# Local attention and two MLPs: attention's q, k and v loaded two units ahead instead of one

## The chip, the cores and the metric

The kernel runs on one core of one Trainium2 chip. The metric is the device time of one execution in microseconds. The kernel before took 663.96, 665.17 and 665.17 us in three runs; the median is 665.17 us. One more execution was taken with a profile, and all rows below come from it.

## What is computed

Three layers follow each other, in float32. The first is attention over 2 batches, 8 heads, 768 positions and 64 columns a head; a query sees the first `n_global` (8) keys and the last `n_local` (96) keys, with a bias that grows with the distance:

```python
scores = scale * np.matmul(q, k.transpose(0, 1, 3, 2))
keep = is_global | is_local          # pos < n_global, or 0 <= rel < n_local
bias = -slopes[:, None, None] * dist[None, :, :]
scores = np.where(keep, scores + bias, -1000000000.0)
a = np.exp(scores - scores.max(-1)); a = a / (a.sum(-1) + 1e-09)
x = np.matmul(a, v)                  # (2, 8, 768, 64) -> (1536, 512)
```

Then two MLPs work on its 1536 rows of 512 columns:

```python
g = x @ w_gate                       # 512 -> 1536
x = (g * sigmoid(g) * (x @ w_val)) @ w_out
h = x @ w_in                         # 512 -> 2048
out = (h * np.cos(h)) @ w_out2
```

The weights arrive as 64-bit floats; the chip's engines take 32 bits, so the kernel also converts them.

## The kernel before, in words

Attention is cut into 12 units. A unit is one of three chunks of 512 query rows (four tiles of 128 rows) with one of four pairs of heads. A unit needs q (128 x 512 floats), the gathered windows of k (128 x up to 744) and of v (128 x 8 x 128). `load(u)` (L560) issues them on SyncE's DMA queue (SP); v comes last. q and k have two buffers in turn, v has three. Unit 0 is loaded ahead of everything, in the prologue.

The loop of `attn_fast` (L687) goes through steps s. A unit has two groups of two tiles, 24 groups in all, and group g is handled over several steps:

- `S_(g)` in step g: the score matmuls on TensorE (PE, L597), then the bias, the row minimum and the exponential on VectorE (DVE, L610) and ScalarE (ACT, L613).
- `R_(g)` and `N_(g)` in step g + 1: the reciprocal of the row sums on DVE, and the division by them on GpSimd (POOL, L626).
- `T_(g)` and `V_(g)` in step g + 3: transposes on PE (L638), copies out of the banks on DVE or ACT (L644), and the value matmuls on PE (L660).
- `X_(g)` in step g + 4: the split of a finished unit into a high and a low part, the input of the first MLP (L396, L400).

q is scaled on POOL by `scale(u)` (L579) before a unit's scores: in step 2u - 1, for u from 1. In one step PE's order is transposes, scores, value matmuls. Every engine works through its own list in the order of the program, and so does SP: an instruction that waits holds all behind it.

Between attention's instructions a small planner (`bg_all`, `bg_fill`) puts the conversion of the weights, a piece at a time. Each piece is a 1 MB load of raw 64-bit words (`load64`, L174), some operations on ACT and DVE that end with L240, and a 512 KB store of the converted tile to memory (`store32`, L245), from which it is read again later. These loads and stores go through the same SP queue as q, k and v. The next raw load is issued right behind the store. The planner counts estimated engine times; `load(u)` tells it of a transfer with `self.dma(1.1)`.

After attention, PE runs the two MLPs almost without a gap, each product as three matmuls of high and low parts (L385 to L387).

The line numbers are those of the kernel before.

Of the kernel before, what the change touches and what calls it, by code (L numbers as in the profile page):

```python
# [18 lines left out]
F32 = mybir.dt.float32  # L19
# [10 lines left out]
CT = 512  # L30
# [3 lines left out]
KC = 744  # L34
# [120 lines left out]
class Body:  # L155
# [399 lines left out]
    def attn_fast(self, p, sc, tr, pv):  # L555
        nc, d = self.nc, self.d
        units = [(c, k) for c in range(NCH) for k in range(NPAIR)]
        op, P, sums, nmins, ptb, pvb = {}, {}, {}, {}, {}, {}

        def load(u):  # L560
            c, k = units[u]
            q = p.tile([128, CT], F32, tag="q", bufs=2, name="q")
            kk = p.tile([128, KC], F32, tag="k", bufs=2, name="kk")
            v = p.tile([128, 8, 128], F32, tag="v", bufs=3, name="v")
            at = 0
            for b in sorted({b for b, _ in TILES[c]}):
                ii = [i for bb, i in TILES[c] if bb == b]
                w = 128 * len(ii)
                nc.sync.dma_start(out=q[:, at:at + w], in_=d["qT"][b, k, :, 128 * ii[0]:128 * ii[0] + w])
                at += w  # L570
            nc.sync.dma_start(out=kk[:, :KW[c]], in_=d["kw"][c, k, :, :KW[c]])
            nc.sync.dma_start(out=v, in_=d["vw"][c, k])
            self.dma(1.1)
            op[u] = (q, kk, v)

        def scale(u):

            q, k = op[u][0], units[u][1]
            nc.gpsimd.tensor_scalar(out=q, in0=q, scalar1=self.qscale[:, k:k + 1], scalar2=1.0,  # L579
                                    op0=ALU.mult, op1=ALU.mult)  # L580
# [7 lines left out]
        def S_(g):  # L588

            u, c, k, tiles = grp(g)  # L590
            q, kk, _ = op[u]
            bank = [sc(), sc()]
            self.at("pe", sum(t[2] for t in tiles) / 500, (), [id(b) for b in bank])
            for i, (t, off, w, vb) in enumerate(tiles):
                for h in range(2):
                    a = slice(64 * h, 64 * h + 64)
                    nc.tensor.matmul(bank[h][:, 256 * i:256 * i + w], lhsT=q[a, 128 * t:128 * t + 128],  # L597
                                     rhs=kk[a, off:off + w], start=True, stop=True)
            sums[g] = p.tile([128, 4], F32, tag="sum", bufs=6, name="sum")
            nmins[g] = p.tile([128, 4], F32, tag="nmin", bufs=6, name="nmin")  # L600
            for i, (t, off, w, vb) in enumerate(tiles):
                dist = self.base[:, 0:128] if w == 128 else self.base[:, 128:128 + WW]
                for h in range(2):
                    n = 2 * i + h
                    pt = p.tile([128, WW], F32, tag="P", bufs=PB, name="P")
                    slope = 2.0 ** -(2 * k + h + 1)
                    nm = nmins[g][:, n:n + 1]

                    self.at("d", w / 700, [id(bank[h])], [("P", g, n)])
                    nc.vector.tensor_tensor_reduce(out=pt[:, :w], in0=bank[h][:, 256 * i:256 * i + w], in1=dist,  # L610
                                                   scale=slope, scalar=3.0e38, op0=ALU.add, op1=ALU.min, accum_out=nm)
                    self.at("a", w / 500, [("P", g, n)], [("P", g, n)])
                    nc.scalar.activation(out=pt[:, :w], in_=pt[:, :w], func=AF.Exp, scale=-1.0, bias=nm,  # L613
                                         accum_out=sums[g][:, n:n + 1])
                    P[g, n] = pt

        def R_(g):
            self.at("d", 0.35, [("P", g, 3)], [("R", g)])
            nc.vector.tensor_scalar_add(sums[g], sums[g], 1.0e-9)
            nc.vector.reciprocal(sums[g], sums[g])  # L620

        def N_(g):
            for i, (t, off, w, vb) in enumerate(grp(g)[3]):
                for n in (2 * i, 2 * i + 1):
                    self.at("g", w / 400, [("R", g)], [("P", g, n)])
                    nc.gpsimd.tensor_scalar(out=P[g, n][:, :w], in0=P[g, n][:, :w], scalar1=sums[g][:, n:n + 1],  # L626
                                            scalar2=1.0, op0=ALU.mult, op1=ALU.mult)

        def T_(g):

            for i, (t, off, w, vb) in enumerate(grp(g)[3]):
                bank = tr()
                nk, nb = (128, 1) if w == 128 else (KB, 2)
                self.at("pe", 0.11 * 2 * nb, [("P", g, 2 * i), ("P", g, 2 * i + 1)], [id(bank)])
                for h in range(2):
                    for j in range(nb):
                        o = 128 * (nb * h + j)
                        nc.tensor.transpose(bank[:nk, o:o + 128], P[g, 2 * i + h][:, nk * j:nk * j + nk], self.ident)  # L638
                    del P[g, 2 * i + h]
                pt = ptb[g, i] = p.tile([128, 512], F32, tag="PT", bufs=PTB, name="PT")  # L640

                e = "a" if self.t["a"] <= self.t["d"] else "d"
                self.at(e, 0.16 + nb * 0.21, [id(bank)], [("E", g, i)])
                (nc.scalar.copy if e == "a" else nc.vector.tensor_copy)(pt[:nk, :256 * nb], bank[:nk, :256 * nb])  # L644

        def V_(g):

            u, c, k, tiles = grp(g)
            v = op[u][2]
            if g % 2 == 0:  # L650
                pvb[u] = pv()
            self.at("pe", 0.25 * sum(len(t[3]) for t in tiles), [("E", g, 0), ("E", g, 1)], [id(pvb[u])])
            for i, (t, off, w, vb) in enumerate(tiles):
                nk = 128 if w == 128 else KB
                pt = ptb.pop((g, i))
                for j, bl in enumerate(vb):
                    for h in range(2):
                        a = slice(64 * h, 64 * h + 64)
                        o = 128 * (len(vb) * h + j)
                        nc.tensor.matmul(pvb[u][a, 128 * t:128 * t + 128], lhsT=v[:nk, bl, a], rhs=pt[:nk, o:o + 128],  # L660
                                         start=j == 0, stop=j == len(vb) - 1)

        def X_(g):

            u, c, k, _ = grp(g)
            if g % 2 == 0:
                return lambda: None
            xt, ps = self.xtile(c, k), pvb.pop(u)
            self.x[c].append(xt)
            self.split_hi(xt, ps)  # L670
            return lambda: self.split_lo(xt, ps)
# [9 lines left out]
        for _ in range(4):  # L681
            nc.tensor.matmul(bank[:, :232], lhsT=zero[:, :128], rhs=zero[:, :232], start=True, stop=True)
        load(1)
        self.bg_start()
        self.distances(p)

        for s in range(NG4 + LAG + 1):  # L687
            self.wr_free = 3 if s > 1 + LAG else 2 if s > 1 else 0
            low = X_(s - LAG - 1) if s > LAG else None
            if LAG <= s < NG4 + LAG:  # L690
                T_(s - LAG)
            if s < NG4:
                if s % 2 == 1 and s // 2 + 1 < len(units):
                    scale(s // 2 + 1)
                S_(s)

            if 1 <= s <= NG4:
                R_(s - 1)
                N_(s - 1)
            if low:  # L700
                low()
            if LAG <= s < NG4 + LAG:
                V_(s - LAG)
            if s % 2 == 0 and 0 < s // 2 < len(units) - 1:
                load(s // 2 + 1)
            yield s

    def attn_general(self, p, banks):
# [199 lines left out]
```

## Time and profile before

| | |
|---|---|
| median of three runs | 665.17 us (663.96 to 665.17) |
| the profiled execution's own time | 664.43 us |
| its span (first to last instruction) | 662.6 us |
| mean granted TensorE clock | 0.993 of full speed |
| PE busy | 635.3 us, 96% of the span |
| DVE, ACT, POOL busy | 66%, 59%, 9% |
| bytes moved | 88.95 MB, mean 134 GB/s |
| attention | from the start to about 97 us |

How to read it: the times in the rows are microseconds from the start of the span. A row of a timeline gives the start, the duration, the engine, the line of the program, the operation, the tiles written and read, and how many instructions were merged; in brackets stands how long the engine was idle before it, and what it waited for. A DMA's issue on SP is short; its data lands later.

### The profile page before, as it was taken

Reading aid. Unit: us, or ns where it says so; the run is one execution under the profiler, and the core shown is the slowest. Engines: PE = TensorE matmul, PEld = TensorE weight load, DVE = VectorE, ACT = ScalarE, POOL = GpSimd, SP = SyncE. Lnnn points to the kernel's source line nnn. Section 1 sums busy time; section 2 is a strip of 40 time slices with the busy share of each in tenths; the row PEclk is TensorE's granted clock in tenths of the full one; section 3 lists DMA queues with packets and bytes.
Section 4 is the critical chain, followed back from the end, with each engine's and each line's share of the span. In section 5 each row is a group of like instructions: output and inputs, shape, how many; then the busy total and the mean of one; then the engine's idle time right before and its main releaser. Section 6 shows DMA issues by size and latency. Waiting matters only on the chain.

```text
span 662.6 us, 8727 instructions
## 1 busy us (share of the span) xinstructions
PE 635.3 (96%) x3176; PEld 517.2 (78%) x3176; DVE 436.8 (66%) x769; ACT 392.7 (59%) x670; POOL 56.7 (9%) x112
## 2 busy tenths in 40 slices
PE   5997989999999999999999998999999999999996
PEld 3674768888888888788888887888888888888885
DVE  4899698787787775557788638766554444554442
ACT  3887575555555454335665348877666665655562
POOL 1676560000000000000000000000000000000000
PEclk9999799999999999999999999999999999999999
DMA  7665425555555455567767442331010000010001
GB/s 261 240 206 212 148 78 208 191 191 194 197 196 197 168 208 196 195 234 258 255 242 251 164 157 65 127 96 32 1 63 1 1 0 1 0 64 0 1 1 68
DMA packets 22658, 88.95 MB, mean 134 GB/s; under 512 B 2640, under 2 KB 3920, under 8 KB 18256
## 3 DMA queue, kind: packets, MB, share of 16 engines
q1 hardware_dynamic: 22176, 88.06, 38.4%
q8 instruction: 27, 0.44, 0.3%
q10 hardware_dynamic: 432, 0.26, 0.1%
q14 instruction: 23, 0.19, 0.1%
HBM read 67.34 MB, written 20.97 MB: 133 GB/s over the span
## 4 chain that ended last, share of the span: by engine, by line
PE 87%; DVE 5%; DMA 3%; ACT 2%; issue 1%; POOL 1%; POOLq 0%; DVEq 0%
PE bank L387 27%; PE bank L385 27%; PE bank L386 27%; PE bank L660 2%; PE bank L597 2%; DMA kk<-in_kw 2%; PE bank L638 2%; DVE P L610 1%; DMA q<-in_qT 1%; DVE PT L644 1%; POOL P L626 0%; DVE x L400 0%; DVE wr L240 0%; DVE w L224 0%; ACT r L475 0%
## 5 line engine op out<-in xcount | busy, mean ns | idle before, releaser
L385 PE MATMUL bank<-x,w 128*128 128x512 f32 x336 | 130.8, 389 | 0.0
L387 PE MATMUL bank<-x,w 128*128 128x512 f32 x336 | 130.7, 389 | 0.0
L386 PE MATMUL bank<-x,w 128*128 128x512 f32 x336 | 130.7, 389 | 0.0
L477 DVE SCALAR_TENSOR_TENSOR u<-r,bank 128x512 f32<-128x512 f32 x48 | 33.0, 688 | 82.3 <-ACT r L475 82.3
L385 PEld LDWEIGHTS bank<-x,w 128*128 128x128 f32 x336 | 63.1, 188 | 13.2 <-issue 0.2
L387 PEld LDWEIGHTS bank<-x,w 128*128 128x128 f32 x336 | 63.1, 188 | 13.1
L386 PEld LDWEIGHTS bank<-x,w 128*128 128x128 f32 x336 | 63.1, 188 | 13.1
L474 ACT ACTIVATE r<-bank,cst 128x512 f32<-128x512 f32 x48 | 33.0, 688 | 47.8 <-PE bank L387 47.8
L387 PE MATMUL bank<-x,big 128*128 128x512 f32 x144 | 56.1, 390 | 1.8 <-DVE big L224 1.8
L385 PE MATMUL bank<-t,w 128*128 128x512 f32 x144 | 56.1, 390 | 0.9 <-ACT w L209 0.9
L387 PE MATMUL bank<-t,w 128*128 128x512 f32 x144 | 56.2, 390 | 0.5 <-DVE w L224 0.5
L613 ACT ACTIVATE P<-P,nmin 128x240 f32<-128x240 f32 (+1 forms) x96 | 44.8, 468 | 20.0 <-DVE nmin L610 20.0
L386 PE MATMUL bank<-t,w 128*128 128x512 f32 x144 | 56.0, 389 | 0.0
L385 PE MATMUL bank<-x,big 128*128 128x512 f32 x144 | 56.0, 389 | 0.0
L385 PE MATMUL bank<-big,g 128*128 128x512 f32 x144 | 56.0, 389 | 0.0
L386 PE MATMUL bank<-big,g 128*128 128x512 f32 x144 | 56.0, 389 | 0.0
L386 PE MATMUL bank<-x,big 128*128 128x512 f32 x144 | 56.0, 389 | 0.0
L387 PE MATMUL bank<-big,g 128*128 128x512 f32 x144 | 56.0, 389 | 0.0
L198 ACT ACTIVATE wr<-r 128x1024 f32<-128x1024 f32 x34 | 39.1, 1149 | 25.5 <-DMA r<-in_gv 11.3
L487 DVE TENSOR_TENSOR r<-bank,r 128x512 f32<-128x512 f32 x48 | 33.1, 690 | 28.5 <-ACT r L486 28.5
L626 POOL TENSOR_SCALAR P<-P,sum 128x240 f32<-128x240 f32 (+1 forms) x96 | 48.4, 523 | 24.4 <-DVE sum L620 21.8
L485 ACT ACTIVATE r<-r 128x512 f32<-128x512 f32 x48 | 30.4, 634 | 33.8 <-DVE r L478 33.6
(79 smaller groups left out, 1159.6 us busy)
## 6 DMA issues: line engine op xcount, KB each, us to landing
scr<-wr SPq DMA_DIRECT2D x34, 512.0 KB, 2.9
r<-in_wo SPq DMA_DIRECT2D x14, 1024.0 KB, 5.7
r<-in_gv SPq DMA_DIRECT2D x12, 1024.0 KB, 5.8
wl<-scr SPq DMA_DIRECT2D x18, 512.0 KB, 4.3
r<-in_win SPq DMA_DIRECT2D x8, 1024.0 KB, 5.7
wr<-scr SPq DMA_DIRECT2D x16, 512.0 KB, 3.3
v<-in_vw SPq DMA_DIRECT2D x11, 512.0 KB, 4.2
out<-wr SPq DMA_DIRECT2D x12, 256.0 KB, 2.4
```

What stands on the lines that cost most here:

```text
L198: self.nc.scalar.activation(out=w, in_=self.raw[n][:, :, 1].bitcast(F32), func=AF.Abs)
L385: mm(out, lhsT=ah, rhs=bh, start=first, stop=False)
L386: mm(out, lhsT=ah, rhs=bl, start=False, stop=False)
L387: mm(out, lhsT=al, rhs=bh, start=False, stop=last)
L474: nc.scalar.activation(out=r, in_=h, func=AF.Identity, scale=INV2PI, bias=self.magic)
L477: nc.vector.scalar_tensor_tensor(out=u, in0=r, scalar=-C1, in1=h, op0=ALU.mult, op1=ALU.add)
L485: nc.scalar.activation(out=r, in_=r, func=AF.Abs)
L487: nc.vector.tensor_tensor(out=r, in0=h, in1=r, op=ALU.mult)
L597: nc.tensor.matmul(bank[h][:, 256 * i:256 * i + w], lhsT=q[a, 128 * t:128 * t + 128], rhs=kk[a, off:off + w], start=True, stop=True)
L613: nc.scalar.activation(out=pt[:, :w], in_=pt[:, :w], func=AF.Exp, scale=-1.0, bias=nm, accum_out=sums[g][:, n:n + 1])
L626: nc.gpsimd.tensor_scalar(out=P[g, n][:, :w], in0=P[g, n][:, :w], scalar1=sums[g][:, n:n + 1], scalar2=1.0, op0=ALU.mult, op1=ALU.mult)
L638: nc.tensor.transpose(bank[:nk, o:o + 128], P[g, 2 * i + h][:, nk * j:nk * j + nk], self.ident)
```

## The change

`load` gets one buffer more for each of q, k and v. The loop issues `load(s // 2 + 2)` in each even step from s = 0 on, where it issued `load(s // 2 + 1)` from s = 2 on. Unit 1 is still loaded ahead of the loop. In both kernels the units 2 to 11 are loaded once each.

```diff
         def load(u):
             c, k = units[u]
-            q = p.tile([128, CT], F32, tag="q", bufs=2, name="q")
-            kk = p.tile([128, KC], F32, tag="k", bufs=2, name="kk")
-            v = p.tile([128, 8, 128], F32, tag="v", bufs=3, name="v")
+            q = p.tile([128, CT], F32, tag="q", bufs=3, name="q")
+            kk = p.tile([128, KC], F32, tag="k", bufs=3, name="kk")
+            v = p.tile([128, 8, 128], F32, tag="v", bufs=4, name="v")
...
             if LAG <= s < NG4 + LAG:
                 V_(s - LAG)
-            if s % 2 == 0 and 0 < s // 2 < len(units) - 1:
-                load(s // 2 + 1)
+
+            if s % 2 == 0 and s // 2 + 2 < len(units):
+                load(s // 2 + 2)
             yield s
```

On DVE, ACT, PE and POOL the operations stand in the same order as before. On SP two places differ. The first is around the store of the first converted weight (`scr0`). In the kernel before SP has there, after unit 8 (`q_976`, `kk_977`, `v_978`), the store, the next raw load, and then unit 9 (`q_1077` and on):

```order
L569 DMA q_976<-in_qT 128x512
L571 DMA kk_977<-in_kw 128x648
L572 DMA v_978<-in_vw 128x1024
L245 DMA scr0_259<-wr0_82 128x1024
L174 DMA r64_1049<-in_gv 128x2048
L569 DMA q_1077<-in_qT 128x512
L571 DMA kk_1078<-in_kw 128x648
L572 DMA v_1079<-in_vw 128x1024
```

In the changed kernel, after unit 8 (`q_886` and on), unit 9 is `q_982`, `kk_983` and `v_984`, and unit 10 begins with `q_1083`:

```order
L569 DMA q_886<-in_qT 128x512
L571 DMA kk_887<-in_kw 128x648
L572 DMA v_888<-in_vw 128x1024
L569 DMA q_982<-in_qT 128x512
L571 DMA kk_983<-in_kw 128x648
L572 DMA v_984<-in_vw 128x1024
L245 DMA scr0_259<-wr0_82 128x1024
L174 DMA r64_1055<-in_gv 128x2048
L569 DMA q_1083<-in_qT 128x512
```

Unit 9 has moved ahead of the store and the raw load; unit 10 now stands straight behind them.

The second place is the start of attention, on SP too: the two first raw loads, unit 2, and unit 3, with the semaphores that each waits for. `PE_49` and `Pool_49` stand for the readers of the buffer that is to be overwritten; a `DMAHW` semaphore belongs to an earlier transfer. Before:

```order
L174 DMA r_319<-in_gv 128x2048 [waits DMAHW1_49]
L174 DMA r_321<-in_gv 128x2048 [waits DMAHW2_49]
L569 DMA q<-in_qT 128x512 [waits DMAHW3_49]
L571 DMA kk<-in_kw 128x640 [waits DMAHW4_49]
L572 DMA v<-in_vw 128x1024 [waits DMAHW5_49]
L569 DMA q<-in_qT 128x512 [waits DMAHW6_49,PE_49,Pool_49]
L571 DMA kk<-in_kw 128x640 [waits DMAHW7_49]
L572 DMA v<-in_vw 128x1024 [waits DMAHW0_49]
```

In the changed kernel:

```order
L174 DMA r_319<-in_gv 128x2048 [waits DMAHW1_49]
L174 DMA r_321<-in_gv 128x2048 [waits DMAHW2_49]
L569 DMA q<-in_qT 128x512 [waits DMAHW3_49]
L571 DMA kk<-in_kw 128x640 [waits DMAHW4_49]
L572 DMA v<-in_vw 128x1024 [waits DMAHW5_49]
L569 DMA q<-in_qT 128x512 [waits DMAHW6_49]
L571 DMA kk<-in_kw 128x640 [waits DMAHW7_49]
L572 DMA v<-in_vw 128x1024 [waits DMAHW0_49]
```

The order is the same; unit 3's q no longer waits for PE and POOL, since its buffer is new.

## Rows read from the trace of the kernel before

**Rows 1.** The page: busy time, share of the span, instructions of an engine.

```profile
PE 635.3 (96%) x3176; PEld 517.2 (78%) x3176; DVE 436.8 (66%) x769; ACT 392.7 (59%) x670; POOL 56.7 (9%) x112
```

**Rows 2.** Stretches: length, busy time per engine (instructions), granted clock, DMA share, GB/s.

```profile
64.00:68.00 4.00, 0.67 (x4) 0.65 (x6) 1.04 (x3) 0.99 (x5) 1.44 (x3) 0.80 1.02 398
68.00:72.00 4.00, 4.00 (x26) 3.03 (x23) 1.81 (x11) 2.13 (x9) 1.74 (x5) 0.50 0.09 30
...
74.00:100.00 26.00, 22.96 (x228) 17.62 (x229) 23.85 (x73) 19.88 (x55) 15.12 (x25) 1.00 0.33 103
100.00:200.00 100.00, 100.00 (x443) 82.84 (x442) 78.84 (x97) 56.81 (x72) 0.00 (x0) 1.00 0.56 197
```

**Rows 3.** Timeline of PE: start, duration, engine, line, operation [idle before, releaser].

```profile
62.58 0.87 PE L638 MATMUL bank<-cst,P 128*128 128x128 f32 x6
67.33 1.97 PE L597 MATMUL bank<-kk,q 64*128 64x240 f32 x8 [3.88 <-POOL q L579]
...
75.96 1.08 PE L597 MATMUL bank<-kk,q 64*128 64x240 f32 x8
...
79.10 1.08 PE L597 MATMUL bank<-kk,q 64*128 64x240 f32 x8
...
97.25 0.50 PE L385 MATMUL bank<-x,w 128*128 128x512 f32 x1
```

**Rows 4.** Timeline of POOL around the scaling of unit 9's q.

```profile
60.91 1.61 POOL L626 TENSOR_SCALAR P<-P,sum 128x128 f32<-128x128 f32 x4 [1.19 <-DVE sum L620]
66.56 0.70 POOL L579 TENSOR_SCALAR q<-q,cst 128x512 f32<-128x512 f32 x1 [4.04 <-DMA q<-in_qT]
```

**Rows 5.** The chain that ended last: start, duration, what; two transfers.

```profile
9.64 10.86 DMA kk<-in_kw
...
59.46 6.92 DMA q<-in_qT
```

**Rows 6.** Timeline of SP: issues of unit 3, of unit 8, and behind it.

```profile
17.68 0.33 SPq L569 DMA_DIRECT2D q<-in_qT  x1
...
47.53 0.33 SPq L569 DMA_DIRECT2D q<-in_qT  x1
...
51.55 0.33 SPq L572 DMA_DIRECT2D v<-in_vw  x1
58.55 0.33 SPq L245 DMA_DIRECT2D scr<-wr  x1
```

**Rows 7.** Timeline of DVE and ACT: conversion's last step, two copies, a raw load's first reader.

```profile
57.30 1.22 DVE L240 TENSOR_TENSOR wr<-wr,se 128x1024 int32<-128x1024 int32 x1
...
64.03 1.01 DVE L644 COPY PT<-bank 128x256 f32<-128x256 f32 x2
...
90.26 1.19 ACT L198 ACTIVATE wr<-r 128x1024 f32<-128x1024 f32 x1
```

**Rows 8.** By tile: issues (min/median/max ns, start) and landing times: r, kk, all q.

```profile
L174 SPq DMA_DIRECT2D r<-in_gv x1: 377/377/377, 59.0 to 59.0; - x1
DMA to landing us min/median/max: 6.0/6.0/6.0
...
L571 SPq DMA_DIRECT2D kk<-in_kw x1: 492/492/492, 60.2 to 60.2; - x1
DMA to landing us min/median/max: 7.0/7.0/7.0
...
  DMA q<-in_qT: 7.8, 3
...
DMA to landing us min/median/max: 2.0/3.6/10.5
```

**Rows 9.** The wait for unit 2's kk: PE's timeline, then the stretch.

```profile
20.64 0.90 PE L597 MATMUL bank<-kk,q 64*128 64x128 f32 x8 [1.24 <-DMA kk<-in_kw]
...
20.00:21.00 1.00, 0.36 (x6) 0.39 (x8) 0.47 (x1) 1.00 (x2) 1.00 (x3) 1.00 1.05 415
```

## The prediction, made before the changed kernel was run

> **What bounds the kernel now.** I read the busy shares first: TensorE (PE) is busy 96% of the span [rows 1]. A gain must therefore come from the few places where PE waits, or where it runs slower than it could. The stretches say where these are. From 74 us on, the granted clock is 1.00 and PE is busy 23.0 of 26 us to the end of attention, then 100 of 100 us [rows 2]. Only one stretch is bad: from 64 to 68 us PE is busy 0.67 of 4 us, and from 68 to 72 us it is busy throughout but at a granted clock of 0.50, the lower of its two levels (1.2 instead of 2.4 GHz) [rows 2].
>
> PE's timeline names the event. Call the score matmuls of group g S(g); a unit u has the groups 2u and 2u+1. Counting the score blocks back from the last, the one at 67.33 us is S(18), the first group of unit 9. PE sat idle 3.88 us before it, and what released it was POOL's scaling of q (L579) [rows 3]. POOL in turn sat idle 4.04 us, until the DMA of q had landed [rows 4]. The chain shows this transfer: 6.92 us from 59.46 us, so it landed at 66.38 us [rows 5].
>
> Why so late? SyncE (SP) issued q, k and v of unit 8 by 51.55 us and nothing more until 58.55 us [rows 6]. There the next instruction in its queue is the store of the first converted weight, and DVE finishes that weight (L240) at 57.30 + 1.22 = 58.52 us [rows 7]. Behind the store comes a 1 MB weight load, and only then unit 9. The weight load landed at 59.0 + 6.0 = 65.0 us; q followed at 66.4, and kk at 60.2 + 7.0 = 67.2 [rows 5, 8]. So unit 9 waited first for its turn to issue, then behind 1.5 MB.
>
> **What the change does, part by part.**
>
> *Order on SP.* Work on the other engines keeps its order; only SP's queue moves. The units up to 8 keep their place in the sequence, but unit 9 now stands ahead of the store and the weight load. Each buffer wait moves with it: with three q buffers the load of unit u waits for S(2u-5), where with two it waited for S(2u-3). So unit 9 is issued when unit 8 was: q at 47.53, v at 51.55 us [rows 6]. A q transfer takes 3.6 us in the median [rows 8], so q lands near 51 us, and even at the longest of all, 10.5 us, near 58, ahead of 62.5 us, where POOL becomes free for it (60.91 + 1.61) [rows 4].
>
> *The stall goes: 3.88 us.* PE ends the transposes before S(18) at 62.58 + 0.87 = 63.45 us [rows 3]. POOL would scale from 62.52 to 63.22 (0.70 us each [rows 4]), so S(18) starts at 63.45 instead of 67.33. Both bounds are close: at least 3.7, if the semaphore from POOL takes some tenths, and at most 3.88.
>
> *The slow clock goes: about 2.0 us.* From S(18) to S(20) the kernel now needs 75.96 - 67.33 = 8.63 us, most of it at half clock; from S(20) to S(21), at full clock, one step is 79.10 - 75.96 = 3.14 us [rows 3], so two are 6.28. That is the low end of what these two steps will cost. The high end has one delay more. The value matmuls after S(18) need copies that DVE makes from 64.03 to 65.04 us [rows 7], while S(18), at 1.08 us as the block at 75.96, ends at 64.53: some 0.57 us of waiting with the semaphore, 6.85 in all. Today the stall covers these copies. I take 6.65, since the value matmuls of that step are 12 and not 16, so part of the wait comes back. Gain 8.63 - 6.65 = 1.98, between 1.78 and 2.35.
>
> *The cover for unit 10.* Unit 10 now stands where unit 9 stood, straight behind the 1 MB load. So its q lands at 66.38 and its kk at 67.2 us, if the store still starts at 58.55, and it does: DVE's part before it is untouched. Is that late? POOL scales q of unit 10 only after two more normalisations: 63.22 + 2 x 1.6 gives 66.4 us at the very earliest with the shortest rows there [rows 4], and really about 68.5, as the second waits for the sums of S(18). S(20) starts near 63.45 + 6.65 = 70.1. Both are in time, POOL by about 2 us and PE by 2.9. Unit 11 comes later still. What was a stall becomes slack.
>
> *The early end.* Unit 3 loses its wait for a q buffer; today its q is issued at 17.68 us [rows 6], and it will follow unit 2 by a few microseconds, while the first two weight loads and unit 2 are under way. The DMA engines are full there (share 1.05, 415 GB/s), and PE waits for kk of unit 2: issued at 9.64, landed 10.86 us later at 20.50, with PE idle 1.24 us before S(4) [rows 5, 9]. If the transfers of one queue land in the order of issue, unit 3 takes nothing from unit 2, and this costs nothing. If all in flight share the engines evenly, the 1.11 MB of unit 3 (128 x 512, 128 x 640 and 128 x 1024 floats) at 415 GB/s cost up to 2.7 us. Landings at 65.0, 66.4 and 67.2 us for issues at 59.0, 59.5 and 60.2 [rows 5, 8] are the nearest rows: they come in the order of issue. I take 0 and keep 2.7 in the range.
>
> The Trainium skill weighs here against order: "DMA: Bandwidth & Descriptors", section "Queues, rings and completion order", says that descriptors on each DMA engine are consumed in ring order, but that completion is not first-in, first-out per issuing engine. By its first half the term is 0, by its second alone a part of the 2.7. The landings above agree with the first half.
>
> *After attention.* Everything from 74 us on waits on other engines or on loads issued behind its own predecessors, so it moves earlier as a block; the weight load that landed at 65.0 is first read by ScalarE at 90.26 us [rows 7]. PE is at 100 of 100 us from 100 us on [rows 2], so nothing there takes the gain back. The larger pool costs no instruction.
>
> **Sum.** 3.88 + 1.98 = 5.86 us. The profiled execution took 664.43 us (span 662.6 and 1.83 around it): 658.6. The median of the three runs is 0.74 higher, which gives 659.3. I forecast 658.9 between them; the likeliest case's own range is 657.6 to 660.2 (gains 5.5 to 6.2, and half a microsecond of spread of the runs).
>
> **Rivals.**
>
> *The clock stays a bound.* PE now runs gapless into S(18), but small waits remain, like the 0.57 us above, and if the clock falls all the same, only the stall is won: 664.43 - 3.88 = 660.6. For it: the clock did fall once in this stage. Against: a wait of 1.24 us left the granted clock at 1.00 [rows 9]; only the wait of 3.88 was followed by a lower one.
>
> *The stall moves to unit 10.* It would come back if the store or the weight load went out later or slower, for instance if the DVE op before the store slid. Each microsecond by which q of unit 10 lands after 68.5 costs about one; landing 3 us late, at 69.4, costs 0.9 plus a tenth or two, so 659.6 to 660.5. Against: the landing times of the same bytes in the same order are known [rows 5, 8].
>
> *Slower: unit 3 takes the engines from unit 2.* Place: 12 to 24 us. If the engines were shared by all in flight, weight loads included, kk of unit 2 would land only with the last of them: v of unit 2, whose 512 KB take 1.3 us more at 415 GB/s, plus 2.7 for unit 3, so 24.5 instead of 20.5. PE would wait 1.24 + 4.0 = 5.2 us, longer than the wait that was followed by the half clock. That clock costs 2.0 as above, up to 2.8 by the stretches (0.20 of 4 us and 0.50 of 4 us [rows 2]). Together 6.0 to 6.8, against a gain of 5.86: 664.6 to 665.4. It decides from a delay of kk of about 3.9 us on. Against: the landings in order.
>
> *The change doesn't reach the late load.* If a wait in unit 9's own instructions still held SP until the store, the time would be 664.4. Against: q of unit 9 now waits for S(13) and its v for unit 5's value matmuls, which are what unit 8's q and v wait for today, and those went out at 47.53 and 51.55 [rows 6].
>
> **Chances.** Forecast 0.75; clock 0.08; stall at unit 10 0.07; slower rival 0.04; no effect, or hidden otherwise, 0.06. A change under 0.2% (1.3 us) is about what a measurement of this kernel cannot tell from none. The first three are all faster, with a part of the others: faster 0.90, same 0.07, slower 0.03. The range reaches over the clock rival and the 2.7 us of the early end in part: 657.2 to 661.8.
>
> **What would show it.** In the profile after: SP issues q, kk and v of unit 9 before the weight store, and its store still near 58.5 us; POOL's waits for a DMA of q fall from three (7.8 us in all [rows 8]) to two; no PE idle over 1.5 us between 55 and 80 us, and the granted clock at 1.00 there; S(20) near 70 instead of 75.96; the first matmul of the first MLP near 91.4 instead of 97.25 [rows 3]; and the stretches after it unchanged in length. I am wrong if S(4) starts later than 20.64, if the clock dips at another place, or if POOL waits for q of unit 10.

## The result, and the profile after

The changed kernel takes 658.88 us (median of four runs, 657.78 to 660.35) against 665.11 us before (four runs, 663.96 to 665.17). The ratio is 0.9911, with a 95% interval of 0.9893 to 0.9929: faster by 6.2 us. The forecast was 658.9 us. The execution with the profile took 657.78 us, with a span of 656.0 us where the kernel before had 662.6.

The two bad stretches are gone. In the stretches of the changed kernel (length, busy time of PE, weight loads, DVE, ACT and POOL with instructions, granted clock, DMA share, GB/s), 64 to 72 us is now like the rest:

```profile
64.00:68.00 4.00, 3.81 (x41) 2.64 (x38) 3.86 (x15) 3.27 (x13) 2.68 (x7) 1.00 1.02 400
68.00:72.00 4.00, 3.99 (x47) 3.09 (x44) 3.78 (x19) 3.26 (x12) 2.86 (x6) 1.00 0.42 169
...
100.00:200.00 100.00, 100.00 (x443) 82.77 (x442) 78.84 (x96) 54.98 (x70) 0.00 (x0) 1.00 0.55 191
```

PE is busy 3.81 of 4 us where it was 0.67, at a clock of 1.00 where it was 0.80 and then 0.50 [rows 2]. The stretch from 100 to 200 us has not changed.

PE's timeline of the changed kernel shows the same blocks as [rows 3]:

```profile
62.37 0.87 PE L638 MATMUL bank<-cst,P 128*128 128x128 f32 x6
63.18 1.08 PE L597 MATMUL bank<-kk,q 64*128 64x240 f32 x8
64.29 0.44 PE L660 MATMUL bank<-PT,v 128*64 128x128 f32 x4
64.89 0.66 PE L660 MATMUL bank<-PT,v 120*64 120x128 f32 x8 [0.16 <-DVE PT L644]
...
69.56 1.08 PE L597 MATMUL bank<-kk,q 64*128 64x240 f32 x8
...
72.69 1.08 PE L597 MATMUL bank<-kk,q 64*128 64x240 f32 x8
...
90.83 0.50 PE L385 MATMUL bank<-x,w 128*128 128x512 f32 x1
```

S(18) follows the transposes without a wait, at 63.18 instead of 67.33 us; S(20) comes at 69.56 instead of 75.96, and the first MLP begins at 90.83 instead of 97.25 us. The 6.4 us won at S(20) are 6.42 us there.

On POOL, q of unit 9 is scaled as soon as POOL is free, with no wait for a DMA in brackets, where [rows 4] has 4.04 us; the last row is q of unit 10, without a wait too:

```profile
60.73 1.60 POOL L626 TENSOR_SCALAR P<-P,sum 128x128 f32<-128x128 f32 x4 [1.22 <-PE bank L597]
62.30 0.69 POOL L579 TENSOR_SCALAR q<-q,cst 128x512 f32<-128x512 f32 x1
...
68.39 0.69 POOL L579 TENSOR_SCALAR q<-q,cst 128x512 f32<-128x512 f32 x1
```

SP's timeline gives the cause. Unit 9 goes out in the place in time that unit 8 had in [rows 6]; the store still goes out near 58.4 us, and the q at 59.26 us behind it is now that of unit 10:

```profile
47.25 0.33 SPq L569 DMA_DIRECT2D q<-in_qT  x1
...
51.30 0.33 SPq L572 DMA_DIRECT2D v<-in_vw  x1
58.35 0.33 SPq L245 DMA_DIRECT2D scr<-wr  x1
...
59.26 0.66 SPq L569 DMA_DIRECT2D q<-in_qT  x1
```

At the early end nothing got worse. By tile (kk of unit 2 alone: issue, then landing; then POOL's waits for q over the whole run), and on PE's timeline:

```profile
L571 SPq DMA_DIRECT2D kk<-in_kw x1: 751/751/751, 9.7 to 9.7; - x1
DMA to landing us min/median/max: 10.6/10.6/10.6
...
  DMA q<-in_qT: 4.4, 2
...
20.37 0.90 PE L597 MATMUL bank<-kk,q 64*128 64x128 f32 x8 [1.52 <-DMA kk<-in_kw]
```

With unit 3 issued from 11.39 us on instead of 17.68, kk of unit 2 lands at 9.7 + 10.6 = 20.3 us (20.5 before), and S(4) starts at 20.37 us (20.64 in [rows 9]). The waits for q are down from three to two.

### The profile page after: what moved, and what is told of

Its sections match the earlier page's. It is cut to its first block, busy times and chain, and to the rows that moved or that the text cites. A ratio compares the mean times of both kernels' runs of the same rounds, so it can differ in the third digit from the quotient of the medians.

```text
span 656.0 us, 8770 instructions
## 1 busy us (share of the span) xinstructions
PE 632.0 (96%) x3176; PEld 514.4 (78%) x3176; DVE 436.1 (66%) x769; ACT 392.4 (60%) x670; POOL 56.4 (9%) x112
## 4 chain that ended last, share of the span: by engine, by line
PE 89%; DVE 5%; ACT 2%; DMA 2%; issue 1%; DVEq 0%
PE bank L387 28%; PE bank L385 27%; PE bank L386 27%; PE bank L660 2%; PE bank L597 2%; PE bank L638 2%; DVE P L610 2%; DMA kk<-in_kw 2%; DVE PT L644 1%; DVE x L400 0%; DVE wr L240 0%; DVE w L224 0%; ACT r L475 0%; ACT w L209 0%; ACT r L474 0%
```

## The experiments

Each comparison is with runs of the kernel before, taken on the same chip together with those of the experiment; the times named below are medians, with their ranges.

**The changed kernel again.** No edit.

> The changed kernel once more, unaltered, with a second profile. Theory (the late load of unit 9 was the cost; stall and slow clock are gone): 657.5 to 660.5 us, S(18) near 63.2 us, no wait of PE over 1.6 us between 55 and 80 us. It also asks for the spread of the first four runs (657.78 to 660.35, where the two longer ones show a mean granted clock of 0.994 and 0.995 and the two shorter 0.999 and 1.0): if a dip of the clock remains in some executions, a profile with a mean clock near 0.995 shows a stretch at 0.50 somewhere in attention, most likely behind the wait for unit 2's kk near 20 us. Rival (the gain is chance of the runs): a ratio whose interval touches 1.

660.34 us (659.17 to 660.50, five runs) against 665.08; ratio 0.9928 (0.9916 to 0.9941). The gain is not chance. The profile had a mean clock of 0.996 and a dip, but not where I had expected it. The wait for unit 2 (1.07 us here) was followed by none. It lay behind a wait of PE of 1.8 us in the second MLP; the stretches of this profile show it, with the granted clock third from the end:

```profile
402.00:404.00 2.00, 1.61 (x5) 1.30 (x6) 1.56 (x3) 1.97 (x5) 0.00 (x0) 0.73 0.30 84
404.00:406.00 2.00, 2.00 (x7) 1.54 (x6) 1.97 (x4) 1.94 (x3) 0.00 (x0) 0.50 0.53 190
```

A third set of runs, on another chip, gave 658.74 us (657.57 to 660.49), ratio 0.9904 (0.9886 to 0.9922):

> The changed kernel a third time, beside the two above on one chip, as the base for differences of a microsecond: 658.5 to 660.5 us, again in two heaps if the dip near 402 us comes in a part of the executions.

Its runs do not lie in two clear heaps (657.57, 657.64, 658.64, 658.84, 659.51, 660.49). Its profiled execution, without the dip, took 657.64 us; the one above, with it, 659.25.

**Only the buffers.** The new buffers, with the loads one unit ahead:

```diff
-            if s % 2 == 0 and s // 2 + 2 < len(units):
-                load(s // 2 + 2)
+            if s % 2 == 0 and 0 < s // 2 < len(units) - 1:
+                load(s // 2 + 1)
```

> The third q and k buffer and the fourth v buffer, but the loads still one unit ahead: the order on all queues is that of the kernel before. Theory: unit 9 still stands behind the store and the 1 MB load, so the wait of PE near 63.5 us stays at 3.9 us, the clock falls to 0.50 behind it, and the time is that of before, 664 to 665.5 us. Rival (the gain comes from waits for buffers that the loads no longer have): the time falls by 2 us or more, to 658 to 663.

664.93 us (664.15 to 665.87), ratio 1.0001 (0.9991 to 1.0011): no gain, as the theory said. PE's timeline and the stretches have the wait and the slow clock of [rows 2, 3] back:

```profile
67.80 1.97 PE L597 MATMUL bank<-kk,q 64*128 64x240 f32 x8 [3.84 <-POOL q L579]
```

```profile
64.00:68.00 4.00, 0.20 (x2) 0.23 (x4) 1.55 (x4) 1.50 (x7) 0.99 (x2) 0.91 1.02 402
68.00:72.00 4.00, 4.00 (x24) 3.01 (x25) 1.66 (x10) 1.66 (x7) 1.69 (x5) 0.50 0.89 355
```

**Only the late units ahead.** The units up to 8 one ahead, from unit 9 on two:

```diff
-            if s % 2 == 0 and s // 2 + 2 < len(units):
+            if s % 2 == 0 and 0 < s // 2 < 8:
+                load(s // 2 + 1)
+            if s % 2 == 0 and 14 <= s <= 18:
                 load(s // 2 + 2)
```

> The new buffers, but only the units from 9 on are issued two ahead; units 2 to 8 are issued one ahead, as before. Of the order on SP only unit 9 ahead of the store and the raw load is left of the change. Theory: the whole gain, 658 to 660 us, S(18) near 63.4 and S(20) near 69.9 us. Rival (the lead of the early units matters too, by a freer DMA queue): half the gain or less, above 661.5 us.

659.46 us (656.95 to 660.92), ratio 0.9914 (0.9895 to 0.9933): the whole gain. PE's timeline has S(18) and S(20) where the changed kernel has them:

```profile
63.19 1.08 PE L597 MATMUL bank<-kk,q 64*128 64x240 f32 x8
...
69.57 1.08 PE L597 MATMUL bank<-kk,q 64*128 64x240 f32 x8
```

**Only the early units ahead.** The units 2 to 8 two ahead, the rest one:

```diff
-            if s % 2 == 0 and s // 2 + 2 < len(units):
+            if s % 2 == 0 and s // 2 + 2 <= 8:
                 load(s // 2 + 2)
+            if s % 2 == 0 and 16 <= s <= 20:
+                load(s // 2 + 1)
```

> The other half: units 2 to 8 two ahead, the units from 9 on one ahead, so unit 9 stays behind the store and the raw load. Theory: no gain, 664 to 665.5 us, the wait of 3.9 us before S(18) as before. Rival (unit 3's early load takes DMA time from unit 2): slower by up to 4 us, with S(4) later than 20.64 us. Rival (early lead is the gain): 661.5 us or less.

665.38 us (664.63 to 667.44), ratio 1.0008 (0.9996 to 1.0020): no gain, and no loss that can be measured. On PE's timeline S(4) is not late, and the wait of [rows 3] stands:

```profile
19.62 0.90 PE L597 MATMUL bank<-kk,q 64*128 64x128 f32 x8 [0.82 <-DMA kk<-in_kw]
...
66.55 1.97 PE L597 MATMUL bank<-kk,q 64*128 64x240 f32 x8 [4.02 <-POOL q L579]
```

These three runs settle that the gain is in the place of the units 9 to 11 on SP; within intervals of 0.1 to 0.2% the buffers alone and the early units give nothing. Which of the late units it is, the run with unit 9 between the store and the raw load shows below.

**The wait kept, the idleness filled.** The kernel before, with matmuls that nothing reads ahead of S(18):

```diff
                 T_(s - LAG)
+            if s == 18:
+                spare = sc.items[sc.n % 4]
+                for _ in range(16):
+                    nc.tensor.matmul(spare[:, :128], lhsT=self.ident, rhs=self.ident, start=True, stop=True)
```

> The kernel before with 16 more 128x128 matmuls on PE just ahead of S(18), written to a bank that S(18) overwrites; nothing reads them. They fill most of the 3.9 us in which PE waits for unit 9, so the wait for the data stays and only the idleness goes. Theory (the second part of the gain was the slow clock behind the wait): the granted clock stays at 1.00 from 64 to 74 us, S(18) stays near 67.3, S(20) comes near 73.7 instead of 75.96, and the time falls by 2.0 to 2.4 us against before, to 662.7 to 663.1 on a median of 665.1. Rival (the steps behind the wait are bound by DVE or POOL, and the slow clock is only seen): same as before, within 0.6 us.

663.11 us (661.65 to 664.50) against 664.74; ratio 0.9972 (0.9959 to 0.9985). PE's timeline, in which the 16 matmuls stand as 32 records:

```profile
62.80 3.74 PE L695 MATMUL bank<-cst 128*128 128x128 f32 x32
67.46 1.08 PE L597 MATMUL bank<-kk,q 64*128 64x240 f32 x8 [0.93 <-DMA kk<-in_kw]
...
73.35 1.08 PE L597 MATMUL bank<-kk,q 64*128 64x240 f32 x8
```

The data come as late as before, at 67.46 us, yet S(18) to S(20) takes 5.89 us instead of 8.63, with the granted clock at 1.00 throughout. The slow clock behind the wait therefore costs time by itself, without the wait. Its size is 2.7 us in this profile (661.71 us, one of the shortest of the twelve runs) and 1.6 us in the medians, whose interval (0.0015 to 0.0041 of 664.74: 1.0 to 2.7 us) holds the 2.0 to 2.4 expected.

**Three buffers of v.**

```diff
-            v = p.tile([128, 8, 128], F32, tag="v", bufs=4, name="v")
+            v = p.tile([128, 8, 128], F32, tag="v", bufs=3, name="v")
```

> The changed kernel with three buffers of v as before, q and k with three. v of unit 9 then waits for the value matmuls of group 13, which PE ends near 62.4 us, and the store and the raw load wait behind it on SP. Theory: the store goes out near 62.5 instead of 58.4 us, q of unit 10 lands near 70.6 and its kk near 71.4 us, so S(20) starts near 71.5 instead of 69.6: about 2 us more than the changed kernel, 1 us more again where the clock falls behind this wait; 661.0 to 663.5 us. Rival (only q and k matter, v's buffer is spare): the time of the changed kernel, 658 to 660.5 us.

659.46 us (658.67 to 660.25), ratio 0.9913 (0.9895 to 0.9930): the time of the changed kernel. Here my expectation failed. I had put the value matmuls of group 13 near 62 us; they are those behind S(16), and SP's timeline shows v of unit 9 going out when they end:

```profile
57.88 0.33 SPq L572 DMA_DIRECT2D v<-in_vw  x1
58.30 0.38 SPq L245 DMA_DIRECT2D scr<-wr  x1
```

It is out 0.42 us ahead of the store, which goes out at its old time. The fourth buffer of v is not needed, though the margin is small.

**Unit 9 between the store and the raw load.** The kernel before with two buffers of q and k, four of v, and `load(9)` called just ahead of the raw load that follows the first store:

```diff
+            if i == 0 and self.fast:
+                self.unit9()                 # load(9)
             if i + 2 < N2:
                 self.load64(order[i + 2])
...
-            if s % 2 == 0 and 0 < s // 2 < len(units) - 1:
+            if s % 2 == 0 and 0 < s // 2 < len(units) - 1 and s != 16:
                 load(s // 2 + 1)
```

> The kernel before with loads one unit ahead and two buffers of q and k (four of v, so that the order below is possible); only unit 9 is issued between the first weight store and the 1 MB raw load behind it, instead of after both. Theory: unit 9 still goes out only after the store, near 59 us, but ahead of the raw load, so q lands near 62.2 and kk near 63 us: S(18) starts at 63.2 to 63.6 us as in the changed kernel, and the time is that of the changed kernel within 0.8 us, 658.5 to 661. Rival (the wait for the turn to issue, up to 58.5 us, is what costs, and only a lead of two units cures it): S(18) later than 65 us and 662 us or more.

660.31 us (659.97 to 663.92), ratio 0.9940 (0.9918 to 0.9962). SP's timeline, then PE's (lines are two further on):

```profile
58.04 0.33 SPq L245 DMA_DIRECT2D scr<-wr  x1
58.54 0.33 SPq L571 DMA_DIRECT2D q<-in_qT  x1
...
60.28 0.37 SPq L174 DMA_DIRECT2D r<-in_gv  x1
```

```profile
63.51 1.08 PE L599 MATMUL bank<-kk,q 64*128 64x240 f32 x8 [0.56 <-DMA kk<-in_kw]
...
69.83 1.08 PE L599 MATMUL bank<-kk,q 64*128 64x240 f32 x8 [0.36 <-POOL q L581]
```

Unit 9 still waits for the store until 58.04 us, and its kk is late by 0.56 us only. So a lead of two units was not required. Moving this one unit ahead of the one 1 MB load wins most of the gain: S(20) comes at 69.83 us against 69.56 in the changed kernel, and the medians fall by 4.4 us, between 2.5 and 5.5 by the interval.

**The wait near 402 us filled.** In the changed kernel PE waits there for the low part of a weight; its timeline has

```profile
402.78 0.50 PE L387 MATMUL bank<-x,big 128*128 128x512 f32 x1 [1.79 <-DVE big L224]
```

```diff
             h = hb()
+            if (c, m) == (0, 4):
+                for _ in range(7):
+                    nc.tensor.matmul(h[:, :128], lhsT=self.ident, rhs=self.ident, start=True, stop=True)
```

> The changed kernel with seven more 128x128 matmuls on PE at the start of the step of the second MLP where PE waits 1.8 us for a weight (L224), near 402 us; nothing reads them. Three of five profiles show a clock of 0.50 for some 3 us behind this wait, two do not, and the runs of the changed kernel lie in two heaps, 657.8 to 658.3 with a mean clock of 0.999 to 1.0, and 659.2 to 660.5 with 0.994 to 0.996. Theory (this dip is the spread): no run with a mean clock under 0.998, all runs between 657 and 659 us. Rival (the spread has another cause, in attention): the spread and the clocks stay as in the changed kernel's runs, with a median near 660.

658.58 us (657.81 to 660.88), ratio 0.9905 (0.9886 to 0.9923). In its profile the wait is 0.20 us, and no dip follows:

```profile
402.75 0.50 PE L387 MATMUL bank<-x,big 128*128 128x512 f32 x1 [0.20 <-DVE big L224]
```

The expectation failed for the runs: one took 660.88 us, and three had a mean clock of 0.995. The dip near 402 us is a part of the spread at most; what else makes it is open.

**Unit 2 ahead of the raw loads**, alone and with the filling near 402 us:

```diff
         load(1)
+        load(2, False)
         self.bg_start()
...
-            if s % 2 == 0 and s // 2 + 2 < len(units):
+            if s == 0:
+                self.dma(1.1)
+            if s % 2 == 0 and 2 < s // 2 + 2 < len(units):
```

(`load` gets a second argument; `False` keeps `load` from telling the planner, which hears of it in step 0 as before, so that no other engine's order moves.)

> The changed kernel with unit 2 issued on SP ahead of the first two 1 MB raw weight loads instead of behind them; no other queue changes its order. It takes away the wait of PE for kk of unit 2 (1.0 to 1.6 us before S(4), near 20 us, in all profiles so far). Theory (loads of one queue land in the order of issue, so what stands ahead is what counts): kk of unit 2 lands near 14 us, S(4) starts near 19 instead of 20.4 us, the first raw load lands near 18.5 us, still ahead of its reader near 20, and the time falls 1.0 to 1.5 us below the changed kernel's of this call, to 657.5 to 659.3. Rival (the raw load is late instead, or the DMA engines share): no gain, within 0.5 us of the changed kernel.

> The kernel with unit 2 ahead of the raw loads, and the seven filling matmuls near 402 us as well. Theory: the gains add; no dip of the clock near 402 us and no wait for unit 2: 656.3 to 658.5 us, the fastest of all, and with less spread than the changed kernel's. Rival (the filling matmuls cost what they save): the time of the kernel with unit 2 first.

Alone: 657.94 us (656.97 to 660.78), ratio 0.9896 (0.9876 to 0.9917). With the filling: 657.29 us (656.66 to 658.12), ratio 0.9878 (0.9860 to 0.9896), against 664.99 before and 658.74 for the changed kernel in the same set of runs. On POOL's and then PE's timeline of the kernel with unit 2 first, neither waits for a DMA any more:

```profile
18.26 0.69 POOL L580 TENSOR_SCALAR q<-q,cst 128x512 f32<-128x512 f32 x1
```

```profile
19.36 0.90 PE L598 MATMUL bank<-kk,q 64*128 64x128 f32 x8
```

The wait before S(4), 1.69 us in the changed kernel's profile of this set, is gone from the trace, and the first MLP begins at 90.08 instead of 91.02 us. In the medians the kernel with unit 2 first is 0.8 us below the changed kernel, less than the 1.0 to 1.5 expected, and the one with the filling too 1.45 us, in the expected range and with the smallest spread of the three. But the intervals of all three overlap: the last is the fastest version run, not one that is shown to beat the changed kernel.

## Why the prediction was right

The mechanism was right, and both terms have been shown apart.

- *The late load, not the buffers and not the early units.* Of the orders of issue tried, only those with unit 9 ahead of the raw load are faster. The three kernels with a part of the change leave only the units 9 to 11, and the kernel that moves unit 9 alone past the raw load has most of the gain.
- *The stall, 3.88 us.* S(18) came 4.15 us earlier. Of these, 0.20 were there before (S(17) started at 59.94 instead of 60.14 us), so 3.95 are the stall.
- *The slow clock, 1.98 us.* Measured 8.63 - (69.56 - 63.18) = 2.25, inside the bounds of 1.78 and 2.35. The term was some 0.3 too small: I let the value matmuls behind S(18) wait for both of DVE's copies, but the first four need only the first copy, and PE waited 0.16 us instead of 0.57. The filled kernel shows that this term is the clock's, and splits it: there the same two steps took 5.89 us, so the half clock cost 2.74. The changed kernel needs 6.38, so 0.49 of it is given back; the wait of 0.16 us for the copy, which the stall had covered, is a part of that.
- *The sum.* 5.86 us forecast; the two terms measured 3.95 + 2.25 = 6.20. At S(20) the two profiles are 6.4 us apart, with the 0.20 from before; the profiled times are 6.65 apart (664.43 and 657.78, the shortest of the changed kernel's four runs), and the medians of the three sets of runs 6.2, 4.7 and 6.25. What makes the difference between these is open. Between the two profiles it is not the dip near 402 us, as neither has one; in runs the dip can come with either order of issue: the profile with only the early units ahead has it too.
- *The exact hit is luck.* The median lies within 0.1 us of the 658.9 forecast, but the other two sets of the same kernel gave 660.34 and 658.74 us, and the two terms were 0.3 us too small.
- *Unit 10 in unit 9's old place.* Its q went out at 59.26 us, where unit 9's had gone out at 59.46, and POOL scaled it at 68.39 us without a wait, against 68.5 forecast.
- *The early end, 0.* kk of unit 2 landed at 20.3 us instead of 20.5 with unit 3 issued close behind it, and the kernel with only the early lead was neither faster nor slower. The slower rival is out: in the changed kernel's profile the transfers of q, kk and v of units 2 and 3, issued from 9.20 to 13.37 us, landed at 19.4, 20.3, 21.5, 22.2, 23.0 and 24.2 us, in the order of issue. Of what the Trainium skill states on this ("DMA: Bandwidth & Descriptors", section "Queues, rings and completion order"), these landings agree with the ring order; that completion need not be first-in, first-out per issuing engine is seen in none of them.
- *The clock rival.* In none of the changed kernel's three profiles did the clock fall in attention. But the ground against this rival was too simple. I took a wait of 1.24 us as harmless and one of 3.88 us as not; the runs show that a wait between these sometimes is followed by the slow clock.
- *What the prediction passed over.* It took PE as busy throughout "from 100 us on", but its row ends at 200 us. PE's timeline of the kernel before has a wait behind that, in the second MLP:

```profile
409.22 0.50 PE L387 MATMUL bank<-x,big 128*128 128x512 f32 x1 [1.79 <-DVE big L224]
```

This is the wait near 402 us of the changed kernel. In one of that kernel's three profiles the clock fell behind it, so one sign of being wrong, a dip at another place, did come. It takes nothing from the two terms above.

- *What I got wrong on the way*, in an expectation and not in the prediction, was the place of group 13's value matmuls, which made me overrate the fourth buffer of v.

## What to carry to other kernels

Where a load is late, first look at what stands ahead of it in its queue: here a store that waited for another engine held a small load back, and a 1 MB transfer for later use then ran ahead of it. Issuing only the last three units earlier, which put one of them ahead of both, won what two units of lead for all units won; moving that one alone ahead of the large transfer won most of it. Price a stall of PE with the slow clock behind it; filling the idle time with matmuls that nothing reads tells the two apart.

## What the runs showed of the hardware

The same wait of PE near 402 us (4 to 7 us later in the kernels with the late load), 1.8 us long and in every profile without the filling there, is followed by a granted clock of 0.50 in some executions and not in others: of eleven such profiles (the two kernels' own included) five show it. The profiled executions of the changed kernel with and without it, on two chips, took 659.25 and 657.64 us. In one more profile, that of the buffers alone, a wait of 1.61 us near 15 us was followed by a clock of 0.51 from 16 to 18 us; the same wait, 1.25 us long in the others, was not. The length alone does not decide: waits of 1.59 and 1.69 us near 20 us, in the profiles of the filled kernel before and of the changed kernel's third set, left the clock at 1.00.
